# Softmax sums on TensorE instead of ScalarE's accumulator, with another planned order, in a set-attention kernel followed by a PReLU layer

## The chip, the cores and the metric

The kernel runs on one core of one Trainium2 chip. The metric is device time in microseconds (us); lower is better. Times are medians of runs; the profile is of one execution.

## The reference

For each of 4 batches, 12480 rows of x (128 wide, float32) are pooled by 32 inducing rows, and every row then attends to the 32 pooled rows. The result goes through a layer of width 2048 with a PReLU.

```
def mab(q, kv):
    s = scale * (q @ kv.transpose(0, 2, 1))
    s = s - s.max(-1, keepdims=True)
    a = np.exp(s)
    a /= a.sum(-1, keepdims=True) + 1e-09
    return a @ kv
h = mab(I, x)                 # I: the 32 inducing rows; h: 4 x 32 x 128
out = mab(x, h)               # 4 x 12480 x 128

h = out @ w_in                # 128 -> 2048
g = np.maximum(h, 0.0) + alpha * np.minimum(h, 0.0)
result = g @ w_out            # 2048 -> 128, float32
```

## The kernel before

Each batch is cut into 7 chunks: six of 2048 rows (512 score columns, 1 MB of float32) and one of 192. "2.3" in this document is chunk 3 of batch 2. A chunk goes through these steps, which are also the names of the functions in the code.

First pass, for the pooled rows h: *load* (GpSimd issues the DMA, which also casts float32 to bf16, into a buffer xn), *flip* (VectorE transposes in 32 x 32 blocks, into xt), *scores* (four TensorE matmuls of 512 columns against the inducing rows, laid out block-diagonally in ind_t), *exps* (ScalarE, into e1), *flip_e* (VectorE, e1 to e1t), *sums* (16 TensorE matmuls that add exp times x into one PSUM tile, h_all). The sum of the exponentials is the softmax's divisor: ScalarE's exp instruction adds its outputs up and a second instruction, an accumulator read, writes the sum into esum.

Fold, once for each batch: *f_hp* and *f_es* take h_all and the sums out of PSUM and esum, *f_tot* adds four row groups together on TensorE, *f_norm* divides, *f_flip* puts h into the block-diagonal BH. Then the batch's 32 rows are multiplied by w_in (*f_hwp*, *f_hw*), and the small matrices SP, ZB and WB are made that stand for the whole layer (*f_ha*, *f_st*, *g_base* to *g_zb*; the last matmuls are *g_rs*, *g_ro*, *g_rl*). The kernel replaces the 2048 hidden columns of each row by what the 32 pooled rows give and corrects the few hidden columns whose sign varies; *extent* and *check* test that this holds, and a full computation stands behind a branch, which is not entered here.

Second pass, for each chunk: scores (against BH, reading xt again, which then comes free), exps (into e2), extent (VectorE), *hidden* (8 matmuls), *invert* (VectorE, the reciprocal of the row sums), *relu* (ScalarE), *outs* (20 matmuls into four PSUM tiles), and then the four output quarters. Each quarter leaves PSUM by a *move*: either VectorE multiplies it by the reciprocal on the way (line 880), or ScalarE copies it (line 882) and GpSimd multiplies afterwards in *scale_out* (line 895), or ScalarE does it alone in four scaled copies (line 885, seldom). SyncE then issues the *store* of 1 MB.

The order is made when the kernel is built. The class Plan holds every step as a task with an engine (or a choice of engines), a duration, the tasks that it depends on, the buffers that it takes and gives back, and a due time *prio*; it plays the program through and writes the instructions of each engine in the order found. At run time each engine goes through its own instructions strictly in that order, and an instruction whose input is not there stops all behind it on its engine. So a load stands in GpSimd's queue between the scale_outs, and a flip in VectorE's queue between moves and inverts.

The due times come from a few constants: TA, TB (distance of first-pass and second-pass chunks), TS, WL, LEAD and FB (how early second scores and folds come), XP (how late extents may). RINGS gives the number of buffers of each kind, CAPS how many of the seven PSUM buffers p may serve scores (A first pass, S second), the fold (F) or outputs (O). SLACK, AP, BIAS and LATE steer which engine moves an output quarter: until LATE (in the plan's own time) VectorE's choice is charged BIAS. Fillers are empty matmuls that Plan puts into waits of TensorE.

Of the kernel before, what the change touches and what calls it, by code (L numbers as in the profile page):

```python
# [10 lines left out]
EXP = mybir.ActivationFunctionType.Exp  # L11
# [3 lines left out]
ALU = mybir.AluOpType  # L15
AX = mybir.AxisListType

P = 128
M = 32
G = 4  # L20
NK = 16
# [5 lines left out]

CENTRE = 1.578125
LOW = 0x3FC8
RINGS = dict(xn=10, xt=14, p=7, h=1, e1=3, e1t=3, g=3, ob=5)  # L30
CAPS = dict(A=2, S=3, F=7, O=5)


def bc(ap, dims):

    return bass.AP(tensor=ap.tensor, offset=ap.offset, ap=[ap.ap[0]] + dims)

# [14 lines left out]
        self.off = off  # L52


SLACK = 0.0
FILL = 0.5
LATE = 130.0
AP = -0.2
BIAS = 0.4


class Plan:
# [15 lines left out]
    def __init__(self):  # L78
        self.tasks = []
        self.free = {k: [0.0] * n for k, n in RINGS.items()}  # L80
        self.used = {}
# [3 lines left out]
    def add(self, eng, fn, deps=(), take=(), give=(), prio=0, bytes=0, after=0.0):  # L85
        t = dict(
            eng={eng[0]: eng[1]} if isinstance(eng, tuple) else eng,
            mode=eng[2] if isinstance(eng, tuple) and len(eng) > 2 else None,
            fn=fn, deps=[d for d in deps if d is not None], take=take, give=give,
            prio=prio, bytes=bytes, after=after, end=None, held={}, n=len(self.tasks),  # L90
        )
        self.tasks.append(t)
        return t
# [147 lines left out]
def kernel(  # L241
    ctx: ExitStack,
    tc: tile.TileContext,
    x: bass.AP,
    inducing: bass.AP,
# [5 lines left out]
    nc = tc.nc  # L251
    f32 = mybir.dt.float32
# [3 lines left out]
    B, N, C = x.shape  # L256
    DFF = moe_w_in.shape[1]
    KC = DFF // P
    assert C == P and inducing.shape[0] == M and KC * P == DFF
    scale = 1.0 / math.sqrt(C)  # L260

    chunks = []
# [11 lines left out]
    NCK = len(chunks)  # L274
    EW = off

    const = ctx.enter_context(tc.tile_pool(name="const", bufs=1))
    keep = ctx.enter_context(tc.tile_pool(name="keep", bufs=1))
# [10 lines left out]
    add = plan.add  # L289
    slots, turn = {}, {}  # L290
# [62 lines left out]
    def zeros(_):  # L353
        nc.vector.memset(blank[:], 0.0)
        nc.vector.memset(ind_t[:], 0.0)
        nc.vector.memset(esum[:], 0.0)
        nc.vector.memset(odd, 0)
        nc.vector.memset(ones_b[:], 1.0)
        nc.vector.memset(mask[:], 0.0)
        for a in range(G):  # L360
            nc.vector.memset(mask[a * M : (a + 1) * M, a : a + 1], 1.0)
# [9 lines left out]
    WO = const.tile([P, KC, C], bf16, name="WO")  # L371
    W1 = const.tile([P, KC, C], bf16, name="W1")
    sel = const.tile([P, M], f32, name="sel")
    sel4 = const.tile([P, G, M], f32, name="sel4")
    sel4b = const.tile([P, G, M], bf16, name="sel4b")
    upper = const.tile([P, P], bf16, name="upper")
# [2 lines left out]
    ones_b = const.tile([P, P], bf16, name="ones_b")  # L379
# [19 lines left out]
    def small_dve(_):  # L399
        nc.vector.tensor_reduce(  # L400
            out=sel[:], in_=ident[:].rearrange("p (q k) -> p k q", q=G), axis=AX.X, op=ALU.add
        )
        nc.vector.tensor_copy(out=sel4[:], in_=bc(sel[:], [[0, G], [1, M]]))
        nc.vector.tensor_copy(out=sel4b[:], in_=sel4[:])
        nc.vector.tensor_copy(out=iota[:], in_=iota_i[:])
        nc.vector.memset(ident1[:], 1.0)
        nc.vector.tensor_copy(out=ident1[:, :M], in_=ident[:M, :M])
        nc.vector.memset(ones_f[:], 1.0)
        nc.vector.memset(one16, 1.0)
        nc.vector.tensor_scalar(out=far[:], in0=ident[:], scalar1=-FAR, scalar2=None, op0=ALU.mult)  # L410


        af = ident[:].rearrange("p (g a f) -> p a g f", g=G, f=CAP)
        nc.vector.tensor_reduce(out=afmask[:], in_=af, axis=AX.XY, op=ALU.add)
        nc.vector.tensor_copy(out=sel8[:], in_=bc(sel[:, :CAP], [[0, P // CAP], [1, CAP]]))
        for r in range(2):
            nc.vector.memset(P0[r][:], 0.0)
            nc.vector.memset(BH[r][:], 0.0)
            nc.vector.memset(SP[r][:], 0.0)

    make_slots(dict(
        xn=([P, NK, C], bf16), xt=([P, NK, 2, M, 2], bf16), p=([P, 512], f32), h=([P, 512], f32),
        e1=([P, NK * M], bf16), e1t=([P, NK // 2, M, 2], bf16), g=([P, P], bf16),
        ob=([P, G, NK // 4, C], f32),
# [2 lines left out]
    flags_f = keep.tile([1, B + 1], f32, name="flags_f")  # L427
    h_all = slots["h"][0][:, :C]
    odd = slots["h"][0][:, C : C + M * NK // 2].bitcast(i32)

    scratch = slots["h"][0][:, C + M * NK // 2 :].rearrange("p (n k) -> p n k", k=KC)
    one16 = scratch[:, 0]
    esum = keep.tile([P, B, NCK], f32, name="esum")
    odds = keep.tile([P, 1], f32, name="odds")


# [4 lines left out]
    for b in range(B):  # L441
        s = Batch()
# [5 lines left out]
        bt.append(s)  # L448

    PW = 12.5  # L450
    FB = 20.0
    OB = 0.42
    TA, TS, TB, WL, LEAD = 4.0, 2.4, 5.0, 12, 4

    HOLD = 15.0

# [15 lines left out]
    def act(n):  # L472
        return ("ACT", 0.19 + n * 0.00073)
# [9 lines left out]
    def pool_chunk(s, c, i):  # L483
        prio = dl_a(s.b, c.i)
        v = {}

        def load(_):
            v["xn"] = ring("xn")
            nc.gpsimd.dma_start(  # L489
                out=v["xn"][: c.p, : c.nk, :],  # L490
                in_=x[s.b, c.t0 : c.t0 + c.n, :].rearrange("(p j) c -> p j c", p=c.p),
            )

        def flip(_):
            xT = ring("xt")
            nc.vector.transpose(  # L496
                out=xT[: c.p, : c.nk].rearrange("p k b j e -> p (k b j e)").bitcast(f32),
                in_=v["xn"][: c.p, : c.nk, :].bitcast(f32),
            )
            s.xT[c.i] = xT  # L500

        def scores(_):
            v["sc"] = ring("p", [P, c.w])
            scores_of(v["sc"], c, ind_t, s.xT[c.i])

        def exps(_):
            v["e1"] = ring("e1")
            nc.scalar.activation(  # L508
                out=v["e1"][: c.p, : c.w].rearrange("p (K j e) -> p K j e", j=M, e=2),
                in_=v["sc"][: c.p, :].rearrange("p (K e j) -> p K j e", j=M, e=2),  # L510
                func=EXP, scale=scale, accum_out=esum[: c.p, s.b, c.i : c.i + 1],
            )

        def flip_e(_):
            v["e1t"] = ring("e1t")
            nc.vector.transpose(  # L516
                out=v["e1t"][: c.p, : c.nk // 2].rearrange("p k m e -> p (k m e)").bitcast(f32),
                in_=v["e1"][: c.p, : c.w].bitcast(f32),
            )

        def sums(_):
            if c.i == 0:
                ring("h")
            for k in range(c.nk):
                q = k % G
                nc.tensor.matmul(  # L526
                    h_all[q * M : (q + 1) * M, :],
                    v["e1t"][: c.p, k // 2, :, k % 2],
                    v["xn"][: c.p, k, :],
                    start=(c.i == 0 and k < G),  # L530
                    stop=(c.i == NCK - 1 and k + G >= c.nk) or (c.i == NCK - 2 and k + G >= c.nk and q >= chunks[-1].nk),
                )

        tl = add(("POOL", 0.55), load, take=["xn"], prio=prio, bytes=c.n * C * 4, after=prio - HOLD)
        s.loads.append(tl)
        tf = add(dve(c.nk * 64), flip, [tl], take=["xt"], prio=prio)
        s.flips.append(tf)
        ts = add(("PE", 0.01 + 4 * max(c.w / 2400, 0.05), (P, P)), scores, [tf] + t_blk, take=["p:A"], prio=prio)
        te = add(("ACT", 0.25 + act(c.w)[1]), exps, [ts], take=["e1"], give=[("p", ts)], prio=prio)
        tt = add(dve(c.w // 2), flip_e, [te], take=["e1t"], give=[("e1", te)], prio=prio)  # L540
        return add(
            ("PE", 0.06 + 0.0115 * c.nk, (P, M)), sums, [tt, s.pooled, ones_done], take=["h"] if c.i == 0 else [],
            give=[("xn", tl), ("e1t", tt)], prio=prio,
        )


    def fold_batch(b):
        s = bt[b]
        r = b % 2
        prio = dl_s(b, -1) - FB  # L550
        v = {}

        def sm(name, shape, dtype):
            v[name] = sm_pool.tile(shape, dtype, name=name, tag=name)
            return v[name]
# [5 lines left out]
            nc.scalar.copy(out=sm("hp", [P, C + 1], f32)[:, :C], in_=h_all)  # L561

        def f_es(_):
            nc.vector.tensor_reduce(
                out=v["hp"][:, C : C + 1], in_=esum[:, s.b, :], axis=AX.X, op=ALU.add
            )

        def f_tot(_):
# [57 lines left out]
            )  # L626

        t = t_c = add(act(C), f_hp, [s.pooled], prio=prio)
        t_e = add(("DVE", 0.15), f_es, [s.pooled, t_c, small], prio=prio)
        add(("NONE", 0.0), lambda _: None, [t_c, t_e], give=[("h", s.first_sum)], prio=prio)  # L630
        t = t_tot = add(("PE", 0.31, (P, P)), f_tot, [t, t_e, small], take=["p:F"], prio=prio)
        t_n = add(("DVE", 0.5), f_norm, [t], give=[("p", t_tot)], prio=prio)
# [42 lines left out]
            s.scored.append(ts)  # L675
            return tx, te

        XP = 30.0
        s.extents, s.weighed, s.scored = [], [], []
        for c in chunks:  # L680
            tx, tq = second(c, dl_s(b, c.i))
# [107 lines left out]
        prio = dl_s(b, -1) - FB  # L789
# [178 lines left out]
    small = add(("DVE", 4.0), small_dve, [t], prio=17)  # L968
    for b in range(B):
        s = bt[b]  # L970
# [138 lines left out]
```

## Time and profile before

| what | before |
|---|---|
| median of 3 runs | 156.04 us (155.24 to 156.47) |
| the profiled execution | 156.47 us |
| its span, first to last instruction | 154.4 us |
| mean granted TensorE clock | 0.856 |
| busy: TensorE, VectorE, ScalarE, GpSimd | 110.7, 105.2, 77.7, 85.0 us |
| read from HBM, written | 27.73 MB, 25.56 MB |
| issue of a load of x to its landing, median | 11.2 us |
| issue of a 1 MB store to its landing, median | 6.1 us |

The page gives busy times by engine, the span in 40 slices with a digit for the busy tenths of each, and groups of equal instructions with their count, busy time, mean duration in ns and the idle time of the engine ahead of them with what ended it. The timeline of an engine gives start, duration, engine, line, operation, output<-input, count, and in brackets the engine's idle time ahead and what ended it. PE is TensorE, PEld its weight loads, DVE VectorE, ACT ScalarE, POOL GpSimd, SP SyncE. Matmul durations in the groups are latencies: matmuls overlap.

### The profile page before, as it was taken

The numbers are of one execution on the slowest core, as the hardware profiler recorded it, in microseconds if no ns is written. First come the engines' busy times: TensorE is split into PE (matmuls) and PEld (weight loads), VectorE is DVE, ScalarE is ACT, GpSimd is POOL, SyncE is SP. The second block draws the span as 40 slices with busy tenths as digits, with TensorE's granted clock in tenths as the row PEclk, the third lists the DMA queues.
The fourth block names the chain that finished last, engine by engine and source line by source line (L and its number), as shares of the span: only waits on it lengthen the run. The fifth ranks groups of instructions, "written<-read, shape, count | busy, mean of one in ns | idle before, by whom it ended". The sixth has DMA issues, their size and how long they took to land.

```text
span 154.4 us, 4218 instructions
## 1 busy us (share of the span) xinstructions
PE 110.7 (72%) x1638; PEld 60.4 (39%) x1638; DVE 105.2 (68%) x277; ACT 77.7 (50%) x212; POOL 85.0 (55%) x110
## 2 busy tenths in 40 slices
PE   0039996898979697990998917999995998376300
PEld 0013343445544454540353604645573544244100
DVE  3099963789989896954678359794889675736600
ACT  3001541264766745872256812668988378546300
POOL 7912114920087993967048640465869266998900
PEclk9999999699999968998579995599999599855555
DMA  3999999999999999999999999848596948669992
GB/s 39 209 213 211 212 215 211 217 210 213 212 223 206 323 327 253 350 286 270 251 389 286 212 269 267 308 160 309 175 398 254 352 169 327 247 258 399 407 403 66
DMA packets 18057, 39.78 MB, mean 258 GB/s; under 512 B 1136, under 2 KB 2416, under 8 KB 18032
## 3 DMA queue, kind: packets, MB, share of 16 engines
q0 software_dynamic: 4192, 13.83, 46.5%
q1 hardware_dynamic: 13648, 25.57, 44.3%
q8 instruction: 14, 0.23, 0.6%
q10 hardware_dynamic: 192, 0.07, 0.3%
q14 instruction: 11, 0.09, 0.1%
HBM read 27.73 MB, written 25.56 MB: 345 GB/s over the span
## 4 chain that ended last, share of the span: by engine, by line
DMA 34%; PE 32%; DVE 11%; ACT 6%; issue 6%; POOL 5%; POOLq 0%; ACTq 0%; DVEq 0%
DMA xn<-in_x_dram 34%; PE p L336 18%; POOL ob L895 5%; DVE xt L496 4%; ACT ob L882 4%; PE p L860 4%; PE p L865 3%; PE h L526 2%; ACT e L508 2%; PE p L834 2%; PE p L760 1%; DVE h L606 1%; DVE ob L880 1%; DVE e1t L516 1%; ACT g L852 1%
## 5 line engine op out<-in xcount | busy, mean ns | idle before, releaser
L895 POOL TENSOR_TENSOR ob<-ob,rd 128x512 f32<-128x512 f32 (+1 forms) x69 | 63.9, 950 | 45.3 <-ACT ob L882 34.5
L336 PE MATMUL p<-xt,ind_t 128*128 128x512 bf16 (+1 forms) x112 | 30.3, 399 | 15.8 <-DVE xt L496 11.4
L882 ACT COPY ob<-p 128x512 f32<-128x512 f32 (+1 forms) x69 | 34.2, 546 | 10.6 <-PE p L865 7.8
L496 DVE STREAM_TRANSPOSE xt<-xn 128x1024 f32<-128x1024 f32 (+1 forms) x28 | 29.9, 1079 | 10.2 <-DMA xn<-in_x_dram 10.1
L508 ACT ACTIVATE e<-p 128x512 bf16<-128x512 f32 (+1 forms) x28 | 15.2, 545 | 29.2 <-PE p L336 22.0
L336 PE MATMUL p<-xt,bh 128*128 128x512 bf16 (+1 forms) x112 | 28.4, 386 | 1.3 <-DVE bh L344 0.6
L880 DVE TENSOR_TENSOR ob<-p,rd 128x512 f32<-128x512 f32 (+1 forms) x37 | 22.7, 645 | 0.2 <-DVE rd L845 0.2
L489 POOL DMA_DIRECT2D xn<-in_x_dram x28 | 15.7, 562 | 10.6 <-DMA xn<-in_x_dram 7.8
L336 PEld LDWEIGHTS <-ind_t 128*128 128x128 bf16 (+1 forms) x112 | 10.2, 109 | 27.4 <-issue 11.6
L655 ACT ACTIVATE e<-p 128x512 bf16<-128x512 f32 (+1 forms) x28 | 15.2, 547 | 8.5 <-PE p L336 8.1
L860 PE MATMUL p<-zb,e 32*128 32x128 bf16 (+1 forms) x396 | 12.4, 242 | 6.5 <-ACT g L852 6.4
L336 PEld LDWEIGHTS <-bh 128*128 128x128 bf16 (+1 forms) x112 | 10.4, 111 | 13.0 <-issue 4.7
L526 PE MATMUL h<-xn,e1t 128*32 128x128 bf16 x392 | 10.4, 232 | 5.7 <-DVE h L664 5.6
L664 DVE SCALAR_TENSOR_TENSOR h<-e,h 128x256 int32<-128x256 int32 (+1 forms) x28 | 10.7, 380 | 4.4 <-ACT e L655 2.8
L516 DVE STREAM_TRANSPOSE e1t<-e 128x256 f32<-128x256 f32 (+1 forms) x28 | 10.7, 388 | 4.0 <-ACT e L508 3.7
L860 PEld LDWEIGHTS <-e 32*128 32x128 bf16 (+1 forms) x396 | 7.7, 102 | 12.5 <-issue 11.5
L845 DVE RECIPROCAL rd<-p 128x16 f32<-128x16 f32 (+1 forms) x28 | 6.6, 237 | 8.3 <-PE p L839 4.6
L865 PE MATMUL p<-wb,g 32*128 32x512 bf16 (+1 forms) x108 | 12.2, 425 | 0.0
L852 ACT ACTIVATE g<-p 128x128 bf16<-128x128 f32 (+1 forms) x28 | 7.7, 276 | 8.7 <-DVE rd L845 8.5
L834 PE MATMUL p<-e,sp 128*128 128x128 bf16 (+1 forms) x100 | 11.4, 238 | 0.0
L526 PEld LDWEIGHTS <-e1t 128*32 128x32 bf16 x392 | 6.7, 101 | 10.7 <-DVE e1t L516 5.5
L834 PEld LDWEIGHTS <-sp 128*128 128x128 bf16 (+1 forms) x100 | 6.5, 104 | 7.4 <-issue 6.2
(105 smaller groups left out, 112.5 us busy)
## 6 DMA issues: line engine op xcount, KB each, us to landing
out_dram<-ob SPq DMA_DIRECT2D x24, 1024.0 KB, 6.1
xn<-in_x_dram POOLq DMA_DIRECT2D x24, 512.0 KB, 11.2
w_in_b<-in_moe_w_in_dram POOLq DMA_DIRECT2D x1, 512.0 KB, 15.1
WO<-in_moe_w_out_dram POOLq DMA_DIRECT2D x1, 512.0 KB, 18.2
out_dram<-ob SPq DMA_DIRECT2D x4, 96.0 KB, 5.8
xn<-in_x_dram POOLq DMA_DIRECT2D x4, 48.0 KB, 9.6
ind<-in_inducing_dram ACTq DMA_DIRECT2D x4, 16.0 KB, 3.0
al<-in_moe_alpha_dram SPq DMA_DIRECT2D x1, 8.0 KB, 1.9
```

Of the source, the lines that this page charges most:

```text
L336: nc.tensor.matmul(sc[: c.p, :], rows_t[: c.p, bb, : c.na, :, e], xT[: c.p, : c.nk, bb, :, e], start=(n == 0), stop=(n == 3),)
L489: nc.gpsimd.dma_start(out=v["xn"][: c.p, : c.nk, :], in_=x[s.b, c.t0 : c.t0 + c.n, :].rearrange("(p j) c -> p j c", p=c.p),)
L496: nc.vector.transpose(out=xT[: c.p, : c.nk].rearrange("p k b j e -> p (k b j e)").bitcast(f32), in_=v["xn"][: c.p, : c.nk, :].bitcast(f32),)
L508: nc.scalar.activation(out=v["e1"][: c.p, : c.w].rearrange("p (K j e) -> p K j e", j=M, e=2), in_=v["sc"][: c.p, :].rearrange("p (K e j) - ...
L526: nc.tensor.matmul(h_all[q * M : (q + 1) * M, :], v["e1t"][: c.p, k // 2, :, k % 2], v["xn"][: c.p, k, :], start=(c.i == 0 and k < G), sto ...
L655: nc.scalar.activation(out=s.e2[: c.p, c.off : c.off + c.w].rearrange("p (r j k) -> p r j k", j=M, k=c.nkk), in_=w["sc"][: c.p, :].rearran ...
L834: nc.tensor.matmul(hh[:, : c.po], SP[r][: c.p, q].rearrange("p a q f -> p (a q f)"), e2(q), start=(q == 0), stop=(q == c.nq - 1),)
L860: nc.tensor.matmul(v["o"][a][: c.po, q * C : (q + 1) * C], e2(q, rows[a]), ZB[r][rows[a], :], start=(q == 0), stop=False,)
L865: nc.tensor.matmul(v["o"][a][: c.po, : c.nq * C], v["g"][rows[a], : c.po], WB[r][rows[a], : c.nq].rearrange("p q c -> p (q c)"), start=Fal ...
L880: nc.vector.tensor_tensor(out=ob, in0=o, in1=spread(rd), op=ALU.mult)
L882: nc.scalar.copy(out=ob, in_=o)
L895: nc.gpsimd.tensor_tensor(out=ob, in0=ob, in1=spread(s.rd[: c.po, c.i, : c.nq, a]), op=ALU.mult,)
```

## The change

The sums of the exponentials are made by TensorE: in *sums*, 8 further matmuls of 64 columns for a full chunk (2 for a small one) multiply a block of ones with e1t and add into 64 further columns of the PSUM tile, e_all. The exp loses its accumulator output, esum goes, and f_es takes from e_all, with the mask sel_e and an accumulating VectorE instruction, what it took from esum. The matmuls with x, 16 in a chunk, stay as they are.

With it go other constants of the plan, and so another order on every engine. The number of buffers xn goes from 10 to 12 and of xt from 14 to 10. The core of the diff:

```diff
-RINGS = dict(xn=10, xt=14, p=7, h=1, e1=3, e1t=3, g=3, ob=5)
-CAPS = dict(A=2, S=3, F=7, O=5)
+RINGS = dict(xn=12, xt=10, p=7, h=1, e1=3, e1t=3, g=3, ob=5)
+CAPS = dict(A=3, S=3, F=7, O=5)
...
-SLACK = 0.0
+SLACK = 0.7
 FILL = 0.5
-LATE = 130.0
-AP = -0.2
-BIAS = 0.4
+LATE = 100.0
+AP = 0.0
+BIAS = 0.8
...
-    FB = 20.0
+    FB = 100.0
     OB = 0.42
-    TA, TS, TB, WL, LEAD = 4.0, 2.4, 5.0, 12, 4
+    TA, TS, TB, WL, LEAD = 4.0, 1.2, 3.4, 6, 2
...
-                func=EXP, scale=scale, accum_out=esum[: c.p, s.b, c.i : c.i + 1],
+                func=EXP, scale=scale,
...
+            for k in range(c.nk // 2):
+                q = k % G
+                nc.tensor.matmul(
+                    e_all[q * M : (q + 1) * M, :], ones_b[: c.p, :M],
+                    v["e1t"][: c.p, k].rearrange("p m e -> p (m e)"),
+                    start=False, stop=...,
+                    skip_group_check=True,
+                )
...
-        te = add(("ACT", 0.25 + act(c.w)[1]), exps, [ts], ...)
+        te = add(("ACT", 0.04 + act(c.w)[1]), exps, [ts], ...)
-            ("PE", 0.06 + 0.0115 * c.nk, (P, M)), sums, ...
+            ("PE", 0.08 + 0.013 * c.nk, (P, M)), sums, ...
...
         def f_es(_):
-            nc.vector.tensor_reduce(
-                out=v["hp"][:, C : C + 1], in_=esum[:, s.b, :], axis=AX.X, op=ALU.add
+            nc.vector.scalar_tensor_tensor(
+                out=sm("junk", [P, 2 * M], f32)[:], in0=e_all, scalar=1.0, in1=sel_e[:],
+                op0=ALU.mult, op1=ALU.mult, accum_out=v["hp"][:, C : C + 1],
             )
...
-        XP = 30.0
+        XP = 40.0
```

In the changed kernel the new matmuls are line 539 and the multiplications of scale_out line 909. Of the 108 output quarters, VectorE moves 28 (37 before), ScalarE copies 79 for GpSimd to multiply (69 before), and one (two before) goes by ScalarE alone.

More of the change, by code (lines that the diff above doesn't have):

```diff
@@ L355, in zeros @@
         nc.vector.memset(ind_t[:], 0.0)
-        nc.vector.memset(esum[:], 0.0)
         nc.vector.memset(odd, 0)
@@ L373 @@
     sel = const.tile([P, M], f32, name="sel")
+    sel_e = const.tile([P, 2 * M], f32, name="sel_e")
     sel4 = const.tile([P, G, M], f32, name="sel4")
@@ L404, in small_dve @@
         nc.vector.tensor_copy(out=sel4b[:], in_=sel4[:])
+        nc.vector.tensor_copy(
+            out=sel_e[:].rearrange("p (m e) -> p m e", e=2), in_=bc(sel[:], [[1, M], [0, 2]])
+        )
         nc.vector.tensor_copy(out=iota[:], in_=iota_i[:])
@@ L429 @@
     odd = slots["h"][0][:, C : C + M * NK // 2].bitcast(i32)
-    scratch = slots["h"][0][:, C + M * NK // 2 :].rearrange("p (n k) -> p n k", k=KC)
+    e_all = slots["h"][0][:, C + M * NK // 2 : C + M * NK // 2 + 2 * M]
+    scratch = slots["h"][0][:, C + M * NK // 2 + 2 * M :].rearrange("p (n k) -> p n k", k=KC)
     one16 = scratch[:, 0]
-    esum = keep.tile([P, B, NCK], f32, name="esum")
     odds = keep.tile([P, 1], f32, name="odds")
@@ L532, in sums @@
                 )
+            for k in range(c.nk // 2):
[3 more added lines that the diff above has]
+                    v["e1t"][: c.p, k].rearrange("p m e -> p (m e)"),
+                    start=False, stop=(c.i == NCK - 1 and k + G >= c.nk // 2)
+                    or (c.i == NCK - 2 and k + G >= c.nk // 2 and q >= chunks[-1].nk // 2),
+                    skip_group_check=True,
+                )
         tl = add(("POOL", 0.55), load, take=["xn"], prio=prio, bytes=c.n * C * 4, after=prio - HOLD)
@@ L538, in pool_chunk @@
         ts = add(("PE", 0.01 + 4 * max(c.w / 2400, 0.05), (P, P)), scores, [tf] + t_blk, take=["p:A"], prio=prio)
-        te = add(("ACT", 0.25 + act(c.w)[1]), exps, [ts], take=["e1"], give=[("p", ts)], prio=prio)
+        te = add(("ACT", 0.04 + act(c.w)[1]), exps, [ts], take=["e1"], give=[("p", ts)], prio=prio)
         tt = add(dve(c.w // 2), flip_e, [te], take=["e1t"], give=[("e1", te)], prio=prio)
         return add(
-            ("PE", 0.06 + 0.0115 * c.nk, (P, M)), sums, [tt, s.pooled, ones_done], take=["h"] if c.i == 0 else [],
+            ("PE", 0.08 + 0.013 * c.nk, (P, M)), sums, [tt, s.pooled, ones_done], take=["h"] if c.i == 0 else [],
             give=[("xn", tl), ("e1t", tt)], prio=prio,
@@ L628, in fold_batch @@
         t = t_c = add(act(C), f_hp, [s.pooled], prio=prio)
-        t_e = add(("DVE", 0.15), f_es, [s.pooled, t_c, small], prio=prio)
+        t_e = add(("DVE", 0.3), f_es, [s.pooled, t_c, small], prio=prio)
         add(("NONE", 0.0), lambda _: None, [t_c, t_e], give=[("h", s.first_sum)], prio=prio)
```

## The prediction

> **What bounds the kernel now.** I read the slices of the page first, then the two in-order queues that a load passes (GpSimd issues it, VectorE flips it), then the groups by shape. Chunk b.c is chunk c of batch b; which instruction is whose is counted off in each engine's order.
>
> The slices, each 3.86 us:
>
> ```profile
> PE   0039996898979697990998917999995998376300
> PEclk9999999699999968998579995599999599855555
> DMA  3999999999999999999999999848596948669992
> GB/s 39 209 213 211 212 215 211 217 210 213 212 223 206 323 327 253 350 286 270 251 389 286 212 269 267 308 160 309 175 398 254 352 169 327 247 258 399 407 403 66
> ```
>
> The DMA is full until about 97 us (24 slices of 9), then 0.5 to 0.9 until 139 us, then full again for the last stores. A load counts only the bf16 bytes it lands, so 212 GB/s is 424 GB/s read. All traffic needs 27.73 MB / 424 + 25.56 MB / 400 = 129.3 us; with 3.5 us ahead of the first load's stream and 2 us behind the last landing the floor is 135 us. The span is 154.4: some 19 us are DMA time not used, mostly after the last load. By then stores of only 11 of 28 chunks had been issued. Why so few, the timelines of GpSimd, VectorE and TensorE say:
>
> ```profile
> 63.34 0.59 POOL L489 DMA_DIRECT2D xn<-in_x_dram  x1
> 71.57 1.25 DVE L496 STREAM_TRANSPOSE xt<-xn 128x1024 f32<-128x1024 f32 x1 [2.78 <-DMA xn<-in_x_dram]
> 79.14 2.05 POOL L895 TENSOR_TENSOR ob<-ob,rd 128x512 f32<-128x512 f32 x2 [6.43 <-ACT ob L882]
> 81.13 0.59 POOL L489 DMA_DIRECT2D xn<-in_x_dram  x1
> 90.35 1.25 DVE L496 STREAM_TRANSPOSE xt<-xn 128x1024 f32<-128x1024 f32 x1 [4.19 <-DMA xn<-in_x_dram]
> 92.41 0.69 DVE L880 TENSOR_TENSOR ob<-p,rd 128x512 f32<-128x512 f32 x1
> 93.15 1.44 PE L336 MATMUL p<-xt,ind_t 128*128 128x512 bf16 x3 [3.75 <-DVE ob L880]
> 98.70 3.06 POOL L895 TENSOR_TENSOR ob<-ob,rd 128x512 f32<-128x512 f32 x3 [8.21 <-ACT ob L882]
> ```
>
> A load queues on GpSimd behind output multiplications; its flip stands in VectorE's queue ahead of output work. The flip of 3.0 held VectorE until 71.57, with flip_e 2.4 behind it, and TensorE waited 4.0 us for that. The load of 3.3 was issued at 81.13, only after the multiplications of 1.1; its flip held VectorE from 86.16 to 90.35. Behind it stood a cast of fold 2 and the move of 1.3, whose PSUM bank TensorE needed: 3.75 us idle, and outs 1.4 began at 96.9, 12.0 us after outs 1.3. GpSimd stood still for 8.21 us. After that TensorE is the slowest: 11.8 of the 12 us from 100 to 112.
>
> **The change, part by part.** The groups by shape give the prices:
>
> ```profile
> L508 ACT ACTIVATION_READ_ACCUMULATOR e<-p 128x1 f32 x24 | 4.7, 197 | 0.0
> L882 ACT COPY ob<-p 128x512 f32<-128x512 f32 x59 | 32.0, 595 | 9.0 <-PE p L865 7.8 <-issue 0.6 <-POOL ob L895 0.6
> L880 DVE TENSOR_TENSOR ob<-p,rd 128x512 f32<-128x512 f32 x35 | 22.2, 666 | 0.2 <-DVE rd L845 0.2
> L895 POOL TENSOR_TENSOR ob<-ob,rd 128x512 f32<-128x512 f32 x59 | 60.2, 1045 | 44.2 <-ACT ob L882 33.4 <-DVE e1t L516 10.8
> L526 PE MATMUL h<-xn,e1t 128*32 128x128 bf16 x384 | 9.7, 232 | 5.7 <-DVE h L664 5.6 <-DVE e1t L516 0.2
> ```
>
> - Accumulator reads gone: 28 x 0.197 = 5.5 us off ScalarE. Its queue was waiting for TensorE's scores, so I count no time for it.
> - Ten more output quarters go by ScalarE and GpSimd, nine fewer by VectorE, one fewer by ScalarE alone in four pieces: ScalarE +4.5 us, VectorE 8 x 0.666 + 0.28 = -5.6 us, GpSimd 9 x 1.045 + 0.39 = +9.8 us. Until the last load this hides under the DMA (a chunk costs it 2.5 + 2.6 us; three multiplications and a load issue are 3.7 us). Without that cover GpSimd's part counts; from chunk 2.0 on it is 31 against 28 full multiplications, 3.5 us with the small ones.
> - 196 new matmuls, 8 in a full chunk. The nearest row is the 16 of line 526, 0.34 us at full clock and 0.41 us to the last end; 8 of the same price are 0.2 us. Bounds: half of that (64 columns stream, not 128) and 0.31 us (the 16 took 0.61 at half clock). I take 0.2: 5.2 us over all, of which only those of 3.3 to 3.6, 0.7 us, come when TensorE is the bound.
> - The sum at the fold reads PSUM instead of an SBUF column: 0.139 us before; by the 128x16 and 128x256 forms of the same operation 0.18 to 0.41 us, four times, once on the path: under 0.3 us.
> - The order, which is the large part. flip_e 2.4 now stands ahead of the flip of 3.0. Loads 3.3 and 3.4 go out together after the multiplications of 1.1, and the flip of 3.3 comes only after fold 2 and invert 1.5. But loads 2.6, 3.0 and 3.1 stand behind the multiplications of 0.5, not 0.3, 0.4 and 0.5; and only 10 xt buffers mean that a flip waits for a second pass ten chunks back.
>
> Now along the path, from rows of before:
> 1. GpSimd from 42.45: 19 multiplications x 1.045 and 4 issues x 0.59 put the issue of 3.0 at 64.7 if it never starves, 69.2 with the 4.5 us of gaps it had. I take 66: fewer moves wait for VectorE, yet fold 1 begins later (all seven extents of batch 0, 0.41 us each, stand ahead of it). With the 7.6 us that this load took to land, the flip starts at 73.7 (71.57 before). Then flip 1.25, a move 0.67, invert 0.25, relu 0.28: outs 1.1 at 76.3 (77.4).
> 2. To outs 1.3 as before, 7.5 us: 83.8 (84.9).
> 3. Outs 1.4 waits for fold 2's products of hT and w_in, 2.9 us after outs 1.3 in before's rows; no flip stands ahead: 87 (96.9).
> 4. VectorE then has invert, three flip_e, a move, two f_ha and fold 2's rest, 6 us: outs 1.5 at 93 (101.8).
> 5. Flips 3.3 to 3.5, fold 2's last pieces, two extents, a move, two inverts: 7.2 us, 0.5 to the matmul: outs 2.0 at 100.7 (106.9). Load 3.5, behind the multiplications of 1.2, has landed by 95.
> 6. To fold 3's first matmul TensorE has four outs, four hidden, the sums of 3.3 to 3.6 and five scores: 10.1 us, 110.8 (112.3), and outs 2.2 and 2.3, which came later before, are done.
> 7. Fold 3 took 8.9 us to its last matmul; with fewer moves between, 7.5. Then two scores and hidden 3.0, with queueing 3.7 us: outs 3.0 at 122 (129.3).
> 8. From there to the end of the span 25.1 us as before (four multiplications for 3.1, the check, 2.4 us per chunk, the last landing) and the score of 3.5, 1.0, which now comes later: 148.1.
>
> The profiled execution took 156.47 us for the span of 154.4, 2.1 more, and is itself 0.43 above the median. 148.1 + 2.1 is 150.2; against the median 149.8. I say **150.0**.
>
> Two rules of the Trainium skill would change this. "DMA: Bandwidth & Descriptors", the anatomy of a DMA by the GpSimd path, fits 2.0 us + bytes / 436e3 for one DMA: an estimate of 4.4 us for a 1.05 MB load. By it load 3.3, issued at 81.13, would land at 85.5 and its flip would never wait, so that step 3 would win nothing and the sum would stay near 156; the trace shows 9.2 us, because stores share the engines, and the trace decides. "TensorE: Matmul & The Clock Gate", "Wait — 56ns, not 53.3ns?", gives some 25 ns as the least distance between matmul starts, however few columns: eight would be 0.2 us, which speaks against my lower bound; no run here shows the new form.
>
> **Rivals.**
> - *The early end is eaten by the engines (no change).* If GpSimd's 3.5 us more from 2.0 on, TensorE's seven sums of batch 3 (1.4 us) and the clock all fall on the path, 148.1 becomes 153.0 and more: 155. For it: from 112 to 132 all engines were 67 to 86% busy, and the last slices run at half clock. Against: the order leaves two chunks fewer after fold 3.
> - *The load wait moves forward (slower).* Place: GpSimd's queue, loads 2.6 to 3.1 behind the four multiplications of 0.5. These need fold 1's products on TensorE, which stand ahead of outs 0.5. If fold 1 is late, load 3.0 is late, the DMA idles, VectorE stands at the flip of 3.0 with all of batch 1 behind it. Each us beyond 66 costs one; it decides from 72 on (step 8 gives away its 6 us). With fold 1 five us late and the gaps of before, 66 + 5 + 4.5 = 75.5: 148.1 + 9.5 + 2.1 = 160. For it: the extents ahead of fold 1, and 10 xt buffers that tie flips 2.3 on to that fold's second pass. Against: outs 0.4 stands ahead of it, and its three multiplications can run while fold 1 goes on.
> - *The sums alone:* if the moved order does nothing, only the 0.7 us of matmuls and 0.3 us of fold are left: 157.
>
> **How the numbers follow.** The forecast has 0.61, its own range 147 to 153.5 (load 3.0 between 64.7 and 69.2, the matmuls' bounds, 2 us for step 7). The engines 0.14, the moved wait 0.20, the sums alone 0.05. The range reaches to 158.5, where the moved wait begins to lie outside, and down to 146.5. This kernel's measurement can tell about 1%, 154.5 to 157.6. Faster: the forecast and a part of the engines' case, 0.66; same: 0.11; slower: 0.23.
>
> **What would show it.** Right: no wait of VectorE over 2 us for a load between 78 and 95; outs 1.4 about 3 us after outs 1.3; fold 3's first matmul near 111 with outs 2.3 done; the DMA over 0.9 until 100 and stores of 13 chunks issued by then. Eight line 539 matmuls in about 0.2 us. Wrong: load 3.0 issued after 70; a new gap over 3 us on TensorE between 60 and 110; GpSimd without gaps from 100 to 122.

## The result, and the profile after

| | before | after |
|---|---|---|
| median | 156.25 us (155.24 to 159.33, 4 runs) | 150.84 us (150.65 to 151.44, 4 runs) |
| span of the profiled execution | 154.4 us | 148.7 us |
| mean granted TensorE clock | 0.856 | 0.907 |
| busy: TensorE, VectorE, ScalarE, GpSimd | 110.7, 105.2, 77.7, 85.0 us | 106.4, 100.4, 78.4, 94.4 us |

The ratio is 0.968, with an interval of 0.962 to 0.974: faster by some 5 us, and 0.8 us from the forecast. Here and below medians are of all runs, while ratios and intervals leave out executions in the chip's slower state.

The slices of the page after, each 3.72 us:

```profile
PE   0009988698995989869459888999878997566100
PEclk9999999999999689999999996899999999755555
DMA  3999999999999999999999899999999975789991
GB/s 38 203 212 212 209 223 212 212 212 217 208 213 245 211 363 267 327 326 386 257 226 311 231 195 233 270 380 403 368 365 382 384 266 203 289 297 385 373 356 47
```

Where the DMA row of before had 4 to 9 from 97 us on, it now stays at 8 or 9 to 119 us, and 365 to 403 GB/s move in the six slices from 97 us, which are stores that had been missing. A table by stage says which engine had been kept waiting; the columns are stage, its length, the busy us of five engines with their instructions, granted clock, DMA share and GB/s. Before:

```profile
60.00:100.00 40.00, 29.82 (x476) 16.61 (x475) 27.67 (x67) 21.40 (x63) 21.48 (x27) 0.83 1.02 288
100.00:125.00 25.00, 22.89 (x362) 12.86 (x363) 19.16 (x57) 18.20 (x50) 17.12 (x19) 0.93 0.69 259
```

and after:

```profile
60.00:100.00 40.00, 32.40 (x617) 19.11 (x616) 29.50 (x76) 25.70 (x68) 30.19 (x38) 0.96 1.02 285
100.00:125.00 25.00, 22.72 (x427) 13.11 (x424) 18.80 (x59) 19.44 (x50) 19.62 (x22) 1.00 0.96 357
```

From 60 to 100 us GpSimd, the fifth busy number, does 30.2 us of work in place of 21.5: its output multiplications come earlier. The DMA was full there in both. From 100 to 125 us it goes from 0.69 to 0.96, because finished chunks lie ready: stores of 14 chunks were issued by 100 us, of 11 before. The timelines of GpSimd, VectorE and TensorE, put in order of time, show why:

```profile
65.63 1.65 POOL L492 DMA_DIRECT2D xn<-in_x_dram  x3
72.00 0.31 DVE L499 STREAM_TRANSPOSE xt<-xn 96x128 f32<-96x128 f32 x1 [2.84 <-DMA xn<-in_x_dram]
75.37 1.25 DVE L499 STREAM_TRANSPOSE xt<-xn 128x1024 f32<-128x1024 f32 x1 [1.17 <-DMA xn<-in_x_dram]
82.12 1.12 POOL L492 DMA_DIRECT2D xn<-in_x_dram  x2
88.64 0.40 PE L874 MATMUL p<-zb,e 32*128 32x128 bf16 x16
92.37 1.25 DVE L499 STREAM_TRANSPOSE xt<-xn 128x1024 f32<-128x1024 f32 x1 [0.27 <-PE p L336]
102.27 13.12 POOL L909 TENSOR_TENSOR ob<-ob,rd 128x512 f32<-128x512 f32 x13 [2.70 <-DVE e1t L519]
110.99 0.49 PE L584 MATMUL p<-hp,sel 128*128 128x129 f32 x2 [0.82 <-DVE junk L577]
128.49 0.61 PE L874 MATMUL p<-zb,e 32*128 32x128 bf16 x16 [1.27 <-ACT g L866]
```

For comparison, outs 1.4 of the kernel before:

```profile
96.92 0.61 PE L860 MATMUL p<-zb,e 32*128 32x128 bf16 x16
```

The load of 3.0 is the second of the three issued from 65.63; its flip is at 75.37. Load 3.3 is issued at 82.12, a microsecond later than before, and landed at 91.4, as much later (90.3 before). But its flip now stands behind fold 2 and starts at 92.37 without waiting for the load; outs 1.4 ran at 88.64 and no longer at 96.92. The 8.2 us that GpSimd stood still at 98.7 before are gone. So nothing was loaded earlier: work that did not need the load was put ahead of the instruction that did.

The groups by shape after:

```profile
L909 POOL TENSOR_TENSOR ob<-ob,rd 128x512 f32<-128x512 f32 x68 | 69.2, 1048 | 28.6 <-ACT ob L896 15.6 <-DVE rd L859 10.0 <-DVE e1t L519 2.7
L896 ACT COPY ob<-p 128x512 f32<-128x512 f32 x68 | 36.1, 599 | 7.7 <-PE p L879 6.7 <-issue 0.7 <-POOL ob L909 0.3
L894 DVE TENSOR_TENSOR ob<-p,rd 128x512 f32<-128x512 f32 x27 | 17.3, 663 | 0.1
L529 PE MATMUL h<-xn,e1t 128*32 128x128 bf16 x384 | 10.0, 232 | 2.2 <-DVE p L730 1.1 <-DVE e1t L519 0.6 <-DVE h L678 0.4
L539 PE MATMUL h<-e1t,ones_b 128*32 128x64 bf16 x192 | 5.9, 200 | 0.0
```

Moves and multiplications cost a piece what they had cost, and nine more full ones stand on GpSimd. The new matmuls are line 539. Their 5.9 us "busy" and 200 ns are latencies; what they take is read from start to start, below.

### The profile page after: what moved, and what is told of

It reads as the page before. It is cut to its first block, busy times and chain, and to the rows that moved or that the text cites. A ratio compares the mean times of both kernels' runs of the same rounds, so it can differ in the third digit from the quotient of the medians.

```text
span 148.7 us, 4608 instructions
## 1 busy us (share of the span) xinstructions
PE 106.4 (72%) x1833; PEld 59.8 (40%) x1833; DVE 100.4 (68%) x271; ACT 78.4 (53%) x191; POOL 94.4 (63%) x120
## 5 line engine op out<-in xcount | busy, mean ns | idle before, releaser
L909 POOL TENSOR_TENSOR ob<-ob,rd 128x512 f32<-128x512 f32 (+1 forms) x79 | 73.2, 956 | 28.9 <-ACT ob L896 15.9
L896 ACT COPY ob<-p 128x512 f32<-128x512 f32 (+1 forms) x79 | 38.2, 553 | 8.2 <-PE p L879 6.7
L336 PE MATMUL p<-xt,ind_t 128*128 128x512 bf16 (+1 forms) x112 | 28.1, 377 | 13.0 <-DVE xt L499 11.6
L336 PE MATMUL p<-xt,bh 128*128 128x512 bf16 (+1 forms) x112 | 26.9, 364 | 2.8 <-DVE ob L894 1.6
L492 POOL DMA_DIRECT2D xn<-in_x_dram x28 | 15.6, 562 | 10.5 <-DMA xn<-in_x_dram 9.7
L336 PEld LDWEIGHTS <-ind_t 128*128 128x128 bf16 (+1 forms) x112 | 9.7, 104 | 23.0 <-DVE ind_t L344 9.6
L874 PE MATMUL p<-zb,e 32*128 32x128 bf16 (+1 forms) x396 | 11.8, 231 | 9.0 <-ACT g L866 8.5
L894 DVE TENSOR_TENSOR ob<-p,rd 128x512 f32<-128x512 f32 (+1 forms) x28 | 17.6, 650 | 0.1
L336 PEld LDWEIGHTS <-bh 128*128 128x128 bf16 (+1 forms) x112 | 9.5, 102 | 11.6 <-issue 2.7
L678 DVE SCALAR_TENSOR_TENSOR h<-e,h 128x256 int32<-128x256 int32 (+1 forms) x28 | 10.8, 386 | 4.6 <-ACT e L669 2.6
L519 DVE STREAM_TRANSPOSE e1t<-e 128x256 f32<-128x256 f32 (+1 forms) x28 | 10.7, 390 | 3.9 <-ACT e L511 3.8
L529 PE MATMUL h<-xn,e1t 128*32 128x128 bf16 x392 | 10.8, 232 | 2.2 <-DVE p L730 1.1
L879 PE MATMUL p<-wb,g 32*128 32x512 bf16 (+1 forms) x108 | 11.5, 397 | 0.0
## 6 DMA issues: line engine op xcount, KB each, us to landing
w_in_b<-in_moe_w_in_dram POOLq DMA_DIRECT2D x1, 512.0 KB, 15.7
```

What stands on the lines that cost most here:

```text
L336: nc.tensor.matmul(sc[: c.p, :], rows_t[: c.p, bb, : c.na, :, e], xT[: c.p, : c.nk, bb, :, e], start=(n == 0), stop=(n == 3),)
L492: nc.gpsimd.dma_start(out=v["xn"][: c.p, : c.nk, :], in_=x[s.b, c.t0 : c.t0 + c.n, :].rearrange("(p j) c -> p j c", p=c.p),)
L529: nc.tensor.matmul(h_all[q * M : (q + 1) * M, :], v["e1t"][: c.p, k // 2, :, k % 2], v["xn"][: c.p, k, :], start=(c.i == 0 and k < G), sto ...
L874: nc.tensor.matmul(v["o"][a][: c.po, q * C : (q + 1) * C], e2(q, rows[a]), ZB[r][rows[a], :], start=(q == 0), stop=False,)
L879: nc.tensor.matmul(v["o"][a][: c.po, : c.nq * C], v["g"][rows[a], : c.po], WB[r][rows[a], : c.nq].rearrange("p q c -> p (q c)"), start=Fal ...
L894: nc.vector.tensor_tensor(out=ob, in0=o, in1=spread(rd), op=ALU.mult)
```

## The experiments

The experiments ran in three sets, each with runs of the kernel before: the first four, then the wait and the check, then the buffers. Runs of the kernel before lay between 151.5 and 159.8 us in them, so differences under 1 us between runs of different sets are weak.

**The sums alone.** The order and the buffers of before, with the new matmuls and f_es.

```diff
-                func=EXP, scale=scale, accum_out=esum[: c.p, s.b, c.i : c.i + 1],
+                func=EXP, scale=scale,
...
+            for k in range(c.nk // 2):
+                q = k % G
+                nc.tensor.matmul(e_all[q * M : (q + 1) * M, :], ones_b[: c.p, :M], ...)
```

> The order of before on every engine, and in it the new matmuls (line 539's kind), no accumulator reads, the fold reading PSUM. Theory (the moved order makes the gain): no gain; the new matmuls cost about 0.06 us a chunk (sums of 24 took 0.47 us in the changed kernel, of 16 0.41), so 156 to 157 us, ratio to before 1.00 to 1.01. Rival (ScalarE freed from 5.5 us of accumulator reads makes the gain): 151 to 153 us, ratio near 0.97.

157.47 us (155.20 to 157.66, 4 runs) beside 155.63 for the kernel before; ratio 1.022 (0.991 to 1.054). Outs 1.4 stayed at 96.9, outs 3.0 at 129.2. The sums on TensorE win nothing that shows, and the rival's 0.97 lies outside the interval.

**The order alone.** The changed kernel with ScalarE's accumulator put back, that is the same edit backwards.

> The order of the changed kernel on every engine, with ScalarE's accumulator and the fold of before in it. Theory: the gain stays, 150 to 151.5 us, ratio 0.962 to 0.972. Rival (the accumulator reads were the cost): 155 to 157 us, ratio near 1.

148.34 us (147.87 to 150.04, 4 runs), ratio 0.972 (0.954 to 0.991), span 146.3; outs 1.4 at 87.8, outs 3.0 at 121.0. The gain comes with the order, and without the sums it is 1.4 us larger (149.70 for the changed kernel in another set, below; the place of the store buffers, also below, has a part in that).

**Flip 3.3 late.** The kernel before, with one instruction of VectorE moved.

```diff
+        behind(('flip', 24), ('invert', 11))      # flip 3.3 behind invert 1.4
```

> The kernel before with one instruction moved: VectorE's flip of 3.3 stands behind invert 1.4 instead of ahead of fold 2's cast. Nothing else differs. Theory (that flip's wait for its load is what held fold 2 and TensorE): outs 1.4 begins near 89 us instead of 96.9, no gap of TensorE over 2 us from 85 to 95, and 3 to 7 us less, 149.5 to 153 us, ratio 0.955 to 0.98. Rival (the gain comes from the output quarters taken off VectorE, or from the second-pass due times): within 1% of before.

153.63 us (151.92 to 154.39, 10 runs), ratio 0.999 (0.993 to 1.006): no gain, where the theory had named 0.955 to 0.98 and the rival within 1%. At the place itself something was won: outs 1.4 began 6.4 us earlier. Then VectorE and TensorE wait again:

```profile
90.53 0.40 PE L874 MATMUL p<-zb,e 32*128 32x128 bf16 x16
97.52 1.43 DVE L510 STREAM_TRANSPOSE xt<-xn 128x1024 f32<-128x1024 f32 x2 [2.28 <-DMA xn<-in_x_dram]
93.47 0.78 PE L540 MATMUL h<-xn,e1t 128*32 128x128 bf16 x32 [1.85 <-DVE h L678]
```

The flip of 3.5 waits for its load in turn, and TensorE has a gap that it did not have. At outs 2.0 only 3.0 of the 6.4 us are left (103.9 for 106.9); that the rest of the queue is still arranged for the old times is my reading, not shown. The span, 151.5, is 2.9 us under that of the one profiled execution of before, but by the ratio this is no gain.

**Both flips late.** The same, and flip 3.0 behind invert 1.1.

> As the run with flip 3.3 moved, and the flip of 3.0 also moved, behind invert 1.1, so that flip_e 2.4 stands ahead of it. Theory: TensorE's gap of 4 us at 69 to 73 goes too, another 1 to 3 us less: 148 to 152 us, ratio 0.95 to 0.97. Rival (the DMA is full there, so an earlier TensorE only waits for the next load): the same time as with flip 3.3 alone, within 0.5 us.

153.26 us (151.21 to 156.13, 10 runs), ratio 0.988 (0.978 to 0.997), again less than the theory's 0.95 to 0.97. Outs 1.1 came at 72.7, 4.7 us earlier, but outs 1.3 only 1.6 us, and outs 1.4 stood at 90.6, where the first move alone had put it:

```profile
74.08 1.25 DVE L511 STREAM_TRANSPOSE xt<-xn 128x1024 f32<-128x1024 f32 x1 [2.44 <-DMA xn<-in_x_dram]
76.36 0.41 PE L541 MATMUL h<-xn,e1t 128*32 128x128 bf16 x16 [2.46 <-DVE h L679]
```

The wait moved one flip on. By the ratios of this set two moves by hand are worth 1.2%, the new order as a whole 2.8%.

**The wait put back.** The changed kernel, with the issues of loads 3.3 and 3.4 moved on GpSimd.

```diff
+        ahead(('load', 24), ('flip', 24))      # load 3.3 as late as the plan allows
+        ahead(('load', 25), ('flip', 25))      # load 3.4
```

> The changed kernel with two instructions moved on GpSimd: the loads of 3.3 and 3.4 stand right ahead of their flips' places, behind the multiplications of 1.4 and of 1.5, so they are issued near 93 and 98 us instead of 82. Theory (a flip's wait in VectorE's queue is what costs): the flip of 3.3 waits 5 to 8 us in front of fold 2's last pieces and of invert 1.6, and the end moves by 4 to 8 us: 154 to 159 us, the gain lost. Rival (the DMA has slack to take the loads later, the gain came from the due times of the second pass): under 2 us more than the changed kernel.

160.48 us (159.57 to 160.65, 4 runs), ratio 1.052 (1.034 to 1.069), and 10.8 us over the changed kernel in the same set (149.70; 149.38 to 149.97, 4 runs; ratio 0.982, 0.967 to 0.997).

> The changed kernel as it is, for comparison within this set: 149.5 to 151.5 us by the first measurement; against it the other three are read. If the sums on TensorE cost what one chunk shows (0.06 us), it stands within 1 us of its order with ScalarE's accumulator.

```profile
92.64 1.11 POOL L507 DMA_DIRECT2D xn<-in_x_dram  x2
101.71 1.25 DVE L514 STREAM_TRANSPOSE xt<-xn 128x1024 f32<-128x1024 f32 x1 [9.96 <-DMA xn<-in_x_dram]
103.18 0.21 PE L863 MATMUL p<-e,sp 96*128 96x64 bf16 x1 [8.73 <-DVE sp L803]
110.86 0.40 PE L889 MATMUL p<-zb,e 32*128 32x128 bf16 x16
```

The loads went out 11.1 us later than in the changed kernel of this set (81.57), VectorE stood 9.96 us at the flip, fold 2's matrix SP behind it with TensorE waiting 8.73 us. The last row is outs 2.0, which needs nothing of these loads: 110.86 in place of 99.72. The end came 10.8 us later, more than the 4 to 8 expected. So a wait at this place costs its whole length. But batch 3's own work became late with its loads too, so this run doesn't tell what the work held up behind the flip cost by itself.

**The check last.** In both orders TensorE stood some 3 us ahead of outs 3.2 for *check*. Here it is planned last, on the changed kernel and on the order alone.

```diff
-        ("DVE", 2.5), check, ..., take=["p:F"], prio=dl_b(B - 1, NCK - 2),
+        ("DVE", 2.5), check, ..., take=["p:F"], prio=dl_b(B - 1, NCK - 2), after=1000.0,
```

> The changed kernel with the check (2.5 us on VectorE, with one matmul) planned after everything else instead of between extent 3.6 and invert 3.2; the plan then gives VectorE two quarters of 3.1. Theory (TensorE's gap of 3.0 us before outs 3.2 is that check, and the stores after it are late by as much): 1.5 to 2.6 us less than the changed kernel, the check hidden under the last stores. Rival (the last stores are set by the DMA): within 0.7 us of the changed kernel.

> The changed kernel's order with ScalarE's accumulator kept for the sums, and the check planned last: the order's gain without the new matmuls. If the two edits add up: 1.5 to 2.6 us less than the run with the order alone, near 146 us, and within 1 us of the changed kernel with the check last; if the last stores are set by the DMA, near 148.

149.20 us (148.71 to 149.97, 4 runs; ratio 0.980, 0.963 to 0.997) and 147.36 us (146.89 to 147.96, 4 runs; ratio 0.968, 0.952 to 0.985): 0.5 us and 1.0 us less. In the first the last store was issued 2.7 us earlier than in the changed kernel, but landed only 0.5 us earlier: the transfers set the end, as the rival had said. And there the two kernels differed in a way that neither theory had: by the bytes moved, their last 1 MB stores landed 2.79 us apart with TensorE's sums, and 2.59 us with ScalarE's.

**The place of the store buffers.** Without esum and with sel_e and junk, the buffers ob lie elsewhere: at 178304 bytes in each partition in the changed kernel, 128 past a multiple of 512, against 185856, a multiple of 512, before and 177664, also one, in the order alone. An unused tile ahead of them, which are the last of the buffers, shifts them alone:

```diff
+            if k == "ob":
+                ctx.enter_context(tc.tile_pool(name="gap_ob", bufs=1)).tile([P, 384], mybir.dt.uint8, name="gap_ob")
```

> The changed kernel with one unused tile of 384 bytes per partition ahead of the five store buffers, and nothing else: it moves the buffers of the output from 128 bytes past a multiple of 512 to a multiple of 512 in on-chip memory, where they lie in the kernel before. Theory A (the place of the buffers sets the rate of the stores; the softmax sums on TensorE cost little by themselves): the last six stores land about 2.6 us apart instead of 2.8, the last slices of the page read about 400 GB/s instead of 356 to 385, and the time is 1.0 to 1.7 us below the changed kernel's, about 148.4. Theory B (the sums on TensorE cost the 1.4 us by which the changed kernel stands behind the order alone): the tail stays at 2.8 us a store and the time at 149.7.

> The order alone (the changed kernel with ScalarE's accumulator for the softmax sums) with one unused tile of 128 bytes per partition ahead of the store buffers: it moves them from a multiple of 512 to 128 past it, as in the changed kernel. Theory A: the last slices fall from 395 to 405 GB/s to some 360 to 385, and the time rises from 148.3 by 1.0 to 1.7 us, to about 149.7. Theory B: nothing moves, 148.3.

The speed row of the page of the changed kernel with its buffers on a multiple of 512 (the next-to-last numbers are the last stores):

```profile
GB/s 38 191 214 213 213 212 214 213 214 215 209 213 190 211 275 369 258 304 377 253 250 303 360 250 253 305 385 401 334 365 401 407 213 253 283 257 402 409 373 42
```

of the order alone, as it is, on a multiple of 512:

```profile
GB/s 36 197 215 213 212 210 215 213 213 214 212 212 206 180 374 314 329 295 393 269 243 278 339 231 237 257 373 402 350 360 405 405 240 271 285 240 403 405 395 44
```

and of the order alone, moved to 128 past one:

```profile
GB/s 36 190 213 213 212 211 213 213 213 215 210 213 248 220 386 256 307 301 399 267 235 291 284 208 239 276 374 403 382 355 385 383 293 187 287 315 380 372 364 40
```

The rate follows the place and not the sums: 402 and 409 against 380 and 372, where the changed kernel had 385 and 373. From 130 to 142 us a 2 KB packet of the stores took 86.0 ns on average in the changed kernel and 85.0 in the order alone on a multiple of 512, and 88.8 and 88.9 ns off it. The times moved as theory A said, by about 1 us, the low end of its 1.0 to 1.7, which is close to the spread of the runs and is read across sets: 148.73 us (147.94 to 150.19, 6 runs; ratio 0.965, 0.956 to 0.975) against 149.70, and 149.44 us (148.39 to 151.79, 6 runs; 0.969, 0.960 to 0.978) against 148.34.

The Trainium skill has a rule for this, in "DMA: Bandwidth & Descriptors", "How a descriptor splits into AXI transactions": a transfer is cut at addresses that are multiples of 256 bytes, and a start between two of them costs the bytes below it too. An estimate from it is 68 beats in place of 64, 6% more. The packets took 3 to 5% more and the rates fell by 4 to 9%, so the direction agrees and the size roughly. Whether a multiple of 256 is enough for stores no run here shows.

**Load buffers too, and both edits together.**

> The order alone with the block-diagonal check planned last, which measured 147.36, with 256 unused bytes ahead of the load buffers and 256 ahead of the store buffers: the load buffers move from 256 past a multiple of 512 to a multiple of 512, the store buffers stay at one. If the place matters for loads as for stores, the slices before 118 us, in which loads and stores share the DMA engines, move more and the time falls by 1 us or more, below 146.5. If only the store buffers' place matters, 147.4 as before.

> The changed kernel with the block-diagonal check planned last, which measured 149.2 and whose last stores were bound by the transfers, with the store buffers moved to a multiple of 512 by 384 unused bytes. Theory A: the last stores land 2.6 us apart instead of 2.8 and the time falls by 1.3 to 2 us, to 147.2 to 147.9, level with the same kernel with ScalarE's sums (147.36). Theory B (the sums on TensorE cost it): 149.2.

147.82 us (147.04 to 149.34, 6 runs; ratio 0.963, 0.954 to 0.972) for the order alone with the check last and all buffers on multiples of 512: not under 147.36, so the load buffers' place, 256 past a multiple of 512, gives nothing that shows. 148.38 us (147.74 to 149.50, 6 runs; ratio 0.966, 0.957 to 0.974) for the changed kernel with the check last and aligned stores: 0.8 us under 149.20, less than the 1.3 to 2 of theory A, and still 0.6 above its twin with ScalarE's sums. The fastest kernel here is the order alone with the check last, 147.36 us, under before and after both.

## Why the prediction was right, step by step

| step | predicted | measured |
|---|---|---|
| 1 load 3.0 issued; its flip; outs 1.1 | 66; 73.7; 76.3 | 66.2; 75.4; 77.8 |
| 2 outs 1.3 | 83.8 | 84.5 |
| 3 outs 1.4 | 87 | 88.6 |
| 4 outs 1.5 | 93 | 93.9 |
| 5 outs 2.0 | 100.7 | 100.8 |
| 6 fold 3's first matmul | 110.8 | 111.0 |
| 7 outs 3.0 | 122 | 122.3 |
| 8 end of the span | 148.1 | 148.7 |

- *The cause.* The sums alone and the order alone show that the gain is the new order's. Within it the trace has the gain where step 3 put it: no flip stands between VectorE and the output of batch 1, outs 1.4 came 8.3 us earlier than before, and 5.7 us were left in the span. That this place is the cause is shown in part only: the wait put back loses more than the whole gain, but the flips moved by themselves won nothing and 1.2%. No run changes the engines' shares or the due times and leaves the flips, so what those give is open. Most signs named in advance came: no wait of VectorE for a load after 78 us, stores of 14 chunks issued by 100 us (13 named), the DMA at 0.9 or more but for one slice of 0.8, fold 3's first matmul at 111 with outs 2.3 done. Two did not: outs 1.4 came 4.2 us after outs 1.3 and not about 3, and the new matmuls cost less than said.
- *Step 1 was 1.5 us short, and later steps gave it back.* Load 3.0 took 9.2 us to its flip, not the 7.6 carried over; before's own rows give 8.2 (63.34 to 71.57), so 0.6 of it was a misreading. Ahead of it flip 2.6 waited 2.84 us, which the sum did not have. Outs 1.1 to 1.3 then took 6.7 us for 7.5, and steps 4 and 5 together 12.2 for 13.7. Step 3 itself was 4.2 us for 2.9. That these cancelled to 0.3 us at outs 3.0 is luck. Load 3.5 landed at 98.2, not by 95; its flip came at 98.99 and waited for nothing.
- *The new matmuls were priced at 0.2 us for eight, and cost 0.06.* From the first matmul of one chunk's sums to the next chunk's it is 0.234 us with 16 (before) and 0.29 with 24 (after) at full clock, 0.40 and 0.53 at half clock. That is under the lower bound of 0.1: the row of 16 is a latency of 0.22 us and 0.19 us of starts, and a row's duration was scaled where only its starts scale. The Trainium skill's rule of 25 ns between starts ("TensorE: Matmul & The Clock Gate", "Wait — 56ns, not 53.3ns?"), which was put against my bound, would give 0.2, an estimate. The trace shows the eight starting within 0.04 to 0.05 us, four at a time mostly 1 to 6 ns apart, and before's sixteen had already started within 0.19 us. The sum held 0.5 us too much for it.
- *The fold's reading was under 0.3 us, as said:*

```profile
83.36 0.23 DVE L577 SCALAR_TENSOR_TENSOR junk<-h,sel_e 128x64 f32<-128x64 f32 x1
83.51 0.08 DVE L577 DVE_READ_ACCUMULATOR junk<-h,sel_e 128x1 f32 x1
```

- *Step 8 had nearly the right size with the wrong term, which is luck.* It gave 1.0 us to the later score of 3.5. From outs 3.0 to outs 3.6 the changed kernel takes 15.7 us, before 15.6: the score shows no cost there. From outs 3.0 to the end it is 26.4 us in place of 25.1, and nearly all of that lies behind outs 3.6, 10.7 us in place of 9.5, where the stores land more slowly. The place of the buffers, which no row of before could show and the diff does not name, was not priced at all.
- *The rivals.* Sums alone at 157 came out at 157.47 when run, but only in part for the reason given: with the place held equal the sums cost 0.4 us (148.73 against 148.34), 0.3 (149.70 against 149.44) and 0.6 (148.38 against 147.82), the first two across sets. In the run with the sums alone the stores' packets took 89.0 ns, as with the buffers off a multiple of 512. The engines did not eat the gain: GpSimd, priced at 9.8 us more, had 9.4, and from 100 to 125 us it was busy 19.6 of 25. The moved wait did not occur, as load 3.0 went out at 66.2; its price, a microsecond for each, was right when two other loads were made 11 us late.
- *Not counted:* the granted clock from 60 to 100 us rose from 0.83 to 0.96. In the order alone it was 0.91 there with outs 1.4 no later, so I don't put the gain to it; how much it gave is open.

## What to carry to other kernels

In an in-order queue, look for the instruction that waits for a transfer, and ask what stands behind it that doesn't need that transfer: here a whole order planned anew won some 3%, while one and two such moves by hand won nothing and 1.2%, as the wait passed on to the next flip. Price short matmuls by the distance of their starts, not by a row's duration. After an edit that adds or drops a small buffer, compare where the store buffers lie and the rate of the last stores: a kernel that ends in transfers pays for their place.

## What was not expected of the hardware

- Stores from on-chip buffers 128 bytes past a multiple of 512 ran at 372 to 385 GB/s where nothing else moved, and at 402 to 409 on a multiple, with the same instructions in the same order; the packets took 88.8 and 88.9 ns in place of 86.0 and 85.0.
- Eight matmuls of 64 columns, each on 32 columns of the array, together added 0.06 us to a run of sixteen.
